# Sinkhorn attention with Fourier mixing on one core: an opening ranked by its longest path, and unread matmuls in TensorE's gaps

## Chip, cores and metric

The kernel runs on one core of a Trainium2 chip. The metric is the device time in microseconds (us) of one execution. Seven runs of the kernel before have a median of 299.0 us, from 294.36 to 301.5.

## What is computed

For 4 batches and 8 heads, a small 8x8 matrix per head is normalised five times by rows and columns (Sinkhorn). It mixes blocks of keys and values, attention runs within each block of 96 rows, and the result x (4 x 768 x 512) goes through a Fourier mixing and a two-layer MLP:

```python
for _ in range(5):
    P = exp(P - max(P)); P /= sum(P, axis=-1); P /= sum(P, axis=-2)
k_sorted = einsum('bhij,bhjcd->bhicd', P, k_b)
v_sorted = einsum('bhij,bhjcd->bhicd', P, v_b)
attn = softmax(scale * q_b @ k_sorted_b.T)       # within each block
x = attn @ v_sorted_b                            # heads side by side
u = x + real(fft(fft(x, axis=1), axis=2))
un = (u - mean(u)) / sqrt(var(u) + 1e-6)         # over the last axis
out = u + maximum(un @ w_ch1, 0) @ w_ch2
```

## The kernel before

The program is not written in the order in which it runs. Every step is recorded with `P.add` as an operation: the engines that may do it, a cost for each, what it reads and writes, a priority, and the buffers it opens. `Plan.schedule` (L201) then plays these costs forward, engine by engine: an engine takes the ready operation with the lowest priority number, and one that may run on ScalarE (ACT) or VectorE (DVE) goes to the engine that is free first. Loads over 32 KB are given a landing time from `HBM = 330.0` (KB per us) and `DLAT = 2.2`. The list of start times is sorted and the instructions are issued in that order. So the order on each engine is fixed when the kernel is built. On the chip each engine works through its list, and what stands first waits for its inputs while the rest of that list waits behind it.

The opening, for batch 0:

- Loads go out on GpSimd's queue (`load`, L395): k and q of the first four heads ("half 0"), v in two halves, k and q of half 1, then two constant tables; later the tables `cs` and `tab`, k and q of batch 1, the weights w1 and w2, v again for the second half of its rows, and k and q of batches 2 and 3. Small ones (`pack` with the identity, the Sinkhorn matrices) go out on SyncE's queue.
- Sinkhorn (L510 to L525) runs on DVE with five exponentials on ACT. Its result is spread to masks: `psk` (L542) and `bdk` (L547) for the keys, `bdv` (L656, L660) for the values.
- `v_path` (L586): 12 matmuls of 128x512 with the identity sum v over a block; L594 reduces that. `v_mix` (L635, L638): 16 groups of eight matmuls mix the values, and each is evicted to `vsf` (by the helper `copy`, L571) by ACT or DVE.
- `attn` for each pair of heads: `q_copy` and the transposes of q (L826, evicted at L571), `kqt` (L797, evicted to `ks`), `scores` (L851), exponential on ACT (L860), minus one (`em1`, L872 on DVE or L874 on ACT), `av` (L891, needs all 16 groups of `v_mix`), and normalisation on DVE (L902, L905) into `rt`.
- `a_path` (L675 to L747) makes correction rows, which three copies bring to `rb` (L760).
- `dft1` (L919 to L985): sums and differences on DVE (`pmt`, `eo`, `fo`), matmuls L952. `dft2` (L1005, L1012, six tiles of 128 rows, in two groups g of three): `u` (L1020), statistics (L1026, L1028), four small operations on GpSimd ("ln", L1033 to L1042), `un` (L1052, L1056), for batch 0 a transpose on TensorE (L1071) and an eviction into `ut`; for later batches a DMA transpose.
- `mlp(b, g)`: 16 groups of four matmuls 128x384 (L1091) with a ReLU eviction (L1100, L1103), then three tiles of 16 matmuls 128x512 (L1112), an addition into `u` (L1120) and a store of 256 KB on SyncE's queue. There are eight such tiles; this work has the lowest rank and fills TensorE (PE) wherever nothing else is ready.

Attention of batch 1 and `v_path(1)` have ranks between; they may be placed ahead of the first MLP tile too. [...] five in pool "pf", three in pool "pm". The MLP uses "pm".

```python
    at(-75.0, (v_path, (0,)))
    at(-60.0, (bdv_make, ()))
    at(-50.0, (v_mix, (0,)))
    at(-80.0, (attn, (0,)))
    at(-40.0, (a_path, (0,)), (a_rows, (0,)))
    at(-30.0, (dft1, (0,)), (dft2, (0, 0)), (dft2, (0, 1)))
    at(10.0, (make_bdk, (1,)), (attn, (1,)))
```

Of the kernel before, what the change touches and what calls it, by code (L numbers as in the profile page):

```python
# [10 lines left out]
F16 = mybir.dt.float16  # L11
# [10 lines left out]
DM = 512  # L22
# [3 lines left out]
RSC = 1.0 / XSC  # L26
YSC = 1.0 / 32.0
QB = (2, 3)
NK = 193
# [70 lines left out]
class Op:  # L100
    __slots__ = ("n", "costs", "fn", "preds", "succs", "left", "ready", "prio",
                 "vts", "fresh", "nbytes", "end", "start", "eng", "tag")

# [12 lines left out]
class Plan:  # L116
    HBM = 330.0
    DLAT = 2.2
# [12 lines left out]
    def add(self, costs, fn, r=(), w=(), prio=None, nbytes=0, tag="",  # L131
            after=()):
        o = Op()
        o.n = len(self.ops)
        o.costs, o.fn, o.nbytes, o.tag = costs, fn, nbytes, tag
        o.prio = self.prio if prio is None else prio
        o.preds, o.succs, o.vts, o.fresh = set(after), [], [], []
        for k in r:
            o.preds.update(self.wr.get(k, ()))
        for k in w:  # L140
            o.preds.update(self.wr.get(k, ()))
            o.preds.update(self.rd.get(k, ()))
        for k in r:
            self.rd.setdefault(k, []).append(o)
        for k in w:
            if self.rd.get(k):
                self.wr[k] = [o]
                self.rd[k] = []
            else:
                self.wr.setdefault(k, []).append(o)  # L150
        for k in list(r) + list(w):
            v = k if isinstance(k, Buf) else (
                k[0] if isinstance(k, tuple) and isinstance(k[0], Buf)
                else None)
            if v is None or v in o.vts:
                continue
            o.vts.append(v)
            v.users.append(o)
            if v.first is None:
                v.first = o  # L160
                o.fresh.append(v)
            elif v.first is not o:
                o.preds.add(v.first)
        o.preds.discard(o)
        self.ops.append(o)
        return o

    def schedule(self):
# [17 lines left out]
        def slot_time(o, held):  # L186
# [15 lines left out]
            return (None if short else t), short  # L202

        while todo:
            pick = None
            for e in free:
                t = free[e]
                cand = None
                soon = None
                held = set()  # L210
                for o in sorted(avail[e], key=lambda o: (o.prio, o.n)):
                    st = 0.0
                    if o.fresh:
                        st, short = slot_time(o, held)
                        if o.ready[e] <= t + 0.3:
                            held |= short
                        if st is None:
                            continue
                    s = max(o.ready[e], st)
                    if s <= t + 1e-9:  # L220
                        cand = o
                        break
                    elif soon is None or s < soon:
                        soon = s
# [69 lines left out]
def kernel(  # L294
# [97 lines left out]
    def load(dst, src, nbytes, w, prio, eng="POOL", r=(), after=()):  # L392
# [3 lines left out]
                     prio=prio, nbytes=nbytes, tag="load", after=after)  # L396


    slot = {}
    for b in range(B):  # L400
        for hf in range(2):
            base = (0, 4, 4, 0)[b]
            for n, nm in enumerate("kq"):
                slot[nm, b, hf] = base + 2 * hf + n

    def qk16(nm, b, hf):
        return kq[:, slot[nm, b, hf], :].rearrange(
            "p (h r d) -> p h r d", h=4, r=6)

    def load_qk(nm, b, hf, prio):  # L410
        src = {"k": k, "q": q}[nm]
        if nm == "q" and b in QB:
            for h in range(4):
# [3 lines left out]
                    src[b, 4 * hf + h].rearrange("(r p) d -> p r d", r=6),  # L417
                    196608, [("kq", slot[nm, b, hf])], prio + 0.01 * h)
            return
        load(kq[:, slot[nm, b, hf], :].rearrange("p (h x) -> p h x", h=4),  # L420
             src[b, 4 * hf:4 * hf + 4, :, :].rearrange(
                 "h (p r) d -> p h (r d)", r=6), 786432,
             [("kq", slot[nm, b, hf])], prio)

    def hk(g):
        return [("h", g, fc) for fc in range(16)]

    def load_v(t, hf, prio):
# [3 lines left out]
            [("nat", t, hf)] + (hk(0)[8 * hf:8 * hf + 8] if t == 0 else  # L432
                                [("kq", 2 * hf), ("kq", 2 * hf + 1)]), prio)

# [41 lines left out]
    for n, nm in enumerate(("pw", "pack", "vrow", "erow", "rrow")):  # L476
        load_c(nm, -500.0 + n, "SP")
    load_qk("k", 0, 0, -500.0)
    load_qk("q", 0, 0, -499.0)
    load_v(0, 0, -498.0)  # L480
    load_v(0, 1, -497.0)
    load_qk("k", 0, 1, -496.0)
    load_qk("q", 0, 1, -495.0)
    load_c("dtab", -494.0)
    load_c("lt", -493.0)
    load_c("cs", 19.0)
# [92 lines left out]
    def v_path(t):  # L579
        n3 = nat[t].rearrange("p (c d) -> p c d", d=D)  # L580
        psm = Buf("pm", "pf") if t else Buf("pm")
        stage = [("kq", n) for n in range(4)] if t else hk(0)
        for hf in range(2):
# [88 lines left out]
    def a_path(t):  # L672
        pa = Buf("pf")
        bd_, bp_ = Buf("qt"), Buf("qt")
        P.add(pe(0.4), lambda _: nc.tensor.matmul(  # L675
# [33 lines left out]
        px, pr = Buf("pf"), Buf("pf")  # L709
        hi, hi2 = Buf("qt"), Buf("qt")  # L710

# [7 lines left out]
        def f(_):  # L719
            for o in range(2):  # L720
                for par in range(2):
                    cc = slice(0, 129) if par == 0 else slice(129, 257)
                    for c in range(2):
# [7 lines left out]
              r=[pr], w=[hi], tag="rhi")  # L731
        P.add(evac(512), lambda e: copy(e, hi2.ap[0:64, 0:512],
                                        px.ap[0:64]),
              r=[px], w=[hi2], tag="rhi")
        for lo, hi_, o in ((0, 129, 0), (129, 257, 256)):
# [12 lines left out]
            rr[0:64, 1, :].rearrange("p (n m) -> p n m", n=2),  # L748
            hi2.ap[0:64, 0:512].rearrange("p (m n) -> p n m", n=2),
            nlo[0:64], px.ap[0:64].rearrange("p (m n) -> p n m", n=2),  # L750
# [3 lines left out]
    def a_rows(b):  # L754
        o = 32 * (b % 2)
        for dst, src in ((rb[0:32, :], rr[o:o + 32, 0, :]),
                         (rb[32:64, :], rr[64 + o:96 + o, 0, :]),
                         (rb[64:96, :], rr[o:o + 32, 1, :])):
            P.add({"SP": (0.1, 2.3)}, lambda _, dst=dst, src=src:
                  nc.sync.dma_start(dst, src),  # L760
                  r=[("rr", i) for i in (0, 1, 2, 3, 256)], w=["rb"],
                  tag="arow")
# [6 lines left out]
    def q_copy(b, hp):  # L769
# [9 lines left out]
        if not first:  # L779
            c["DVE"] = (0.28, 0.35)  # L780
        P.add(c, lambda e: copy(
            e, qr.ap.rearrange("p r (h d) -> p r h d", h=2), src),
            r=[("kq", slot["q", b, hf])], w=[qr], tag="qcp",
            after=[exps[-1]] if first else [])

    def kqt(b, hp):
# [4 lines left out]
        for half in range(2):  # L791
            ps = Buf("pf")

            def f(_, half=half, ps=ps):
                for r3 in range(3):
                    for h2 in range(2):
# [4 lines left out]
                            bdk[:, 2 * hp + h2].rearrange("p i c -> p (i c)"))  # L801
            P.add(pe(0.22), f, r=[("kq", slot["k", b, hf]),
                                  ("bdk", hp // 2)],
# [8 lines left out]
        if b in QB:  # L812
# [4 lines left out]
                kq[:, slot["q", b, hf], 768 * hl:768 * hl + 768]),  # L817
                r=[("kq", slot["q", b, hf])], w=[qt], tag="qX")
            return
# [60 lines left out]
    def av(b, h):  # L880
# [4 lines left out]
        def f(_):  # L885
            for T in range(6):
# [9 lines left out]
        P.add(pe(0.5), f, r=[(eb, 0), (eb, 1), "erow", "vrow", "vsz"]  # L896
              + [("vsb", n) for n in range(16)], w=[po], tag="av")
        rz = Buf("rz")
# [16 lines left out]
    def dft1(b):  # L915
        rt = rts[b]
        hs = [(rt, h) for h in range(H)]
        for n in range(2):
            P.add({"DVE": (0.86, 0.95)}, lambda _, n=n: V.tensor_tensor(  # L919
                pmt[:, 3 * n:3 * n + 3, 0:DM], rt.ap[:, 0:3, :],  # L920
                rt.ap[:, 3:6, :], op=ALU.add if n == 0 else ALU.subtract),
                r=hs, w=[("pm", n), ("fq", 0), ("fq", 1)],
                tag="pmt")
        P.add({"ACT": (0.17, 0.22)},
              lambda _: nc.scalar.copy(
                  pmt[:, :, DM:DM + 1], pmt[:, :, 0:1]),
              r=[("pm", 0), ("pm", 1)], w=["pm2"], tag="pmc")
        pms = [("pm", 0), ("pm", 1), "pm2"]
        P.add({"DVE": (0.88, 0.97)}, lambda _: V.tensor_tensor(
# [62 lines left out]
    def dft2(b, g):  # L992
# [4 lines left out]
        for tt in range(3):  # L997
# [11 lines left out]
            def f(_, one=one, ps=ps, T=T):  # L1009
                for c in range(4):  # L1010
# [5 lines left out]
                  r=[y4[c][g] for c in range(4)]  # L1016
                  + ["rb", "rrow", "lt", "lt96", "lt96a", "lt96b", "dtab"],
                  w=[ps, u], tag="dft2")
# [24 lines left out]
            nm.ap, nm.ap, -1.0, None, op0=ALU.mult), r=[nm], w=[(nm, 1)],  # L1043
            tag="ln")
        ut = Buf("ut")
        uts[b, g] = ut
        for tt in range(3):
# [20 lines left out]
            def f(_, un=un, pt=pt):  # L1068
                p16 = pt.ap.bitcast(F16)
                for c in range(4):  # L1070
# [9 lines left out]
                          "p (c s) -> p c s", c=4)),  # L1080
                  r=[pt], w=[(ut, tt, 1)], tag="utev")


# [43 lines left out]
    def attn(b):  # L1127
# [5 lines left out]
        for h in range(H):  # L1133
            av(b, h)

    def at(p, *fns):
        for fn, a in fns:
            P.prio = p
            fn(*a)
# [5 lines left out]
    at(-40.0, (a_path, (0,)), (a_rows, (0,)))  # L1145
    at(-30.0, (dft1, (0,)), (dft2, (0, 0)), (dft2, (0, 1)))
    at(10.0, (make_bdk, (1,)), (attn, (1,)))
# [18 lines left out]
    for b in range(B):  # L1166
        for g in range(2):
            mlp(b, g, 100.0 + 10 * (2 * b + g), -300.0)
    with tc.manual_schedule():
        for o in P.schedule():  # L1170
            o.fn(o.eng)
# [28 lines left out]
```

The softmax here doesn't subtract the row's maximum and nothing guards it: scores larger than these inputs give would overflow.

## Time and profile before

| | |
|---|---|
| median of seven runs | 299.0 us (294.36 to 301.5) |
| the profiled execution | 300.14 us, its span 298.4 us |
| PE busy | 269.8 us (90% of the span), 2332 matmuls |
| DVE busy | 177.8 us (60%); 56.70 us of the 65.40 from 10.00 to 75.40 |
| ACT busy | 153.5 us (51%) |
| mean granted TensorE clock | 0.971 |
| first MLP matmul (L1091) starts at | 75.39 us |
| PE busy from 133.80 to 294.50 | 160.55 us of 160.70 |

All times count from the first instruction of the span. "Busy" of PE counts pipelined matmuls that overlap. The granted clock (PEclk) is the share of TensorE's full clock in a stretch. A chain of waits is followed back from the last instruction to what released each step.

### The profile page before, as it was taken

Reading aid. Unit: us, or ns where it says so; the run is one execution under the profiler, and the core shown is the slowest. Engines: PE = TensorE matmul, PEld = TensorE weight load, DVE = VectorE, ACT = ScalarE, POOL = GpSimd, SP = SyncE. Lnnn points to the kernel's source line nnn. Section 1 sums busy time; section 2 is a strip of 40 time slices with the busy share of each in tenths; the row PEclk is TensorE's granted clock in tenths of the full one; section 3 lists DMA queues with packets and bytes.
Section 4 is the critical chain, followed back from the end, with each engine's and each line's share of the span. In section 5 each row is a group of like instructions: output and inputs, shape, how many; then the busy total and the mean of one; then the engine's idle time right before and its main releaser. Section 6 shows DMA issues by size and latency. Waiting matters only on the chain.

```text
span 298.4 us, 5829 instructions
## 1 busy us (share of the span) xinstructions
PE 269.8 (90%) x2332; PEld 165.0 (55%) x2332; DVE 177.8 (60%) x395; ACT 153.5 (51%) x307; POOL 54.7 (18%) x91
## 2 busy tenths in 40 slices
PE   0398978785999999889999999999999999999994
PEld 0264977664556565555556645545645645645641
DVE  5598589999699999776249954314605315312001
ACT  2476579863646897478237604513721631641710
POOL 8945312013800036030002000200200100010000
PEclk9999699996699999999999999999999999999999
DMA  7999999990910359625010210030021121121002
GB/s 115 218 283 218 216 206 213 204 118 13 71 12 2 72 98 165 134 13 108 35 71 15 55 70 35 20 107 36 15 53 70 37 53 70 37 54 70 37 0 105
DMA packets 43025, 26.32 MB, mean 88 GB/s; under 512 B 29834, under 2 KB 38552, under 8 KB 42996
## 3 DMA queue, kind: packets, MB, share of 16 engines
q0 software_dynamic: 22576, 15.16, 33.3%
q1 hardware_dynamic: 20422, 10.78, 12.4%
q8 instruction: 18, 0.29, 0.4%
q14 instruction: 9, 0.07, 0.1%
HBM read 28.95 MB, written 6.29 MB: 118 GB/s over the span
## 4 chain that ended last, share of the span: by engine, by line
PE 73%; DVE 15%; DMA 6%; POOL 2%; ACT 2%; issue 2%; DVEq 0%; ACTq 0%; POOLq 0%
PE bank L1112 28%; PE bank L1091 25%; DMA hr<-in_v_dram 4%; PE bank L635 3%; DVE rt L905 2%; PE bank L1005 2%; PE bank L952 2%; PE bank L851 2%; DMA out_dram<-u 2%; PE bank L891 2%; PE bank L586 2%; DVE pmt L919 2%; PE bank L638 2%; PE bank L797 1%; DVE u L1020 1%
## 5 line engine op out<-in xcount | busy, mean ns | idle before, releaser
L1103 ACT ACTIVATE hr<-bank 128x384 f16<-128x384 f32 x111 | 54.2, 490 | 80.1 <-PE bank L1091 79.8
L1091 PE MATMUL bank<-ut,w1sb 128*128 128x384 f16 x512 | 93.4, 331 | 0.8 <-DVE hr L1100 0.8
L1112 PE MATMUL bank<-w2sb,hr 128*128 128x512 f16 x384 | 88.9, 379 | 0.0
L1091 PEld LDWEIGHTS <-w1sb 128*128 128x128 f16 x512 | 49.5, 99 | 36.0 <-issue 3.0
L1112 PEld LDWEIGHTS <-hr 128*128 128x128 f16 x384 | 36.5, 98 | 40.5
L1120 DVE TENSOR_TENSOR u<-bank,u 128x512 f32<-128x512 f32 x24 | 16.6, 691 | 51.7 <-PE bank L1112 51.3
L1020 DVE SCALAR_TENSOR_TENSOR u<-rt,bank 128x512 f32<-128x512 f16 x24 | 16.1, 678 | 35.4 <-PE bank L1012 29.7
L860 ACT ACTIVATE ex<-bank 96x384 f32<-96x384 f32 x64 | 27.9, 485 | 7.3 <-PE bank L851 5.5
L1033 POOL TENSOR_SCALAR mv<-mv 128x3 f32<-128x3 f32 x8 | 2.6, 320 | 142.2 <-DVE mv L1028 140.0
L1052 ACT ACTIVATE un<-u,nm,ny 128x512 f16<-128x512 f32 x14 | 11.4, 811 | 14.2 <-POOL nm L1042 8.5
L395 POOL DMA_DIRECT2D kq<-in_q_dram x20 | 17.5, 892 | 5.3 <-ACT vsf L571 1.9
L891 PE MATMUL bank<-vsf,eb 97*128 97x65 f16 x384 | 15.8, 195 | 2.7 <-DVE u L1020 1.3
L874 ACT ACTIVATE eb<-ex,negone 96x384 f16<-96x384 f32 x29 | 17.5, 614 | 0.2
L905 DVE TENSOR_TENSOR rt<-bank,rz 128x384 f16<-128x384 f32 x32 | 17.3, 549 | 0.4
L891 PEld LDWEIGHTS <-eb 97*128 97x128 f16 x384 | 14.3, 98 | 4.8 <-issue 2.9
L826 PE MATMUL bank<-pack,qr 128*128 128x128 f16 x48 | 4.9, 252 | 12.6 <-ACT qr L571 11.8
L1026 DVE BATCH_NORM_STATS2 st<-u 128x6 f32<-128x512 f32 x24 | 15.9, 682 | 0.2
L571 ACT CAST vsf<-bank 96x512 f16<-96x512 f32 x19 | 13.9, 786 | 4.1 <-PE bank L638 3.2
L395 POOL DMA_DIRECT2D kq<-in_k_dram x8 | 6.5, 810 | 48.4 <-issue 27.7
L635 PE MATMUL bank<-bdv,vcx 128*128 128x128 f16 (+1 forms) x128 | 14.0, 236 | 1.1 <-ACT bdv L571 1.1
L872 DVE TENSOR_SCALAR eb<-ex 96x384 f16<-96x384 f32 x35 | 13.1, 376 | 1.2 <-ACT ex L860 0.9
L1100 DVE TENSOR_SCALAR hr<-bank 128x384 f16<-128x384 f32 x17 | 9.4, 551 | 5.6 <-PE bank L1091 5.6
(114 smaller groups left out, 336.7 us busy)
## 6 DMA issues: line engine op xcount, KB each, us to landing
out_dram<-u SPq DMA_DIRECT2D x24, 256.0 KB, 2.0
kq<-in_k_dram POOLq DMA_DIRECT2D x8, 384.0 KB, 9.3
w1sb<-in_moe_w_ch_dram POOLq DMA_DIRECT2D x4, 512.0 KB, 15.2
w2sb<-in_moe_w_ch_dram POOLq DMA_DIRECT2D x4, 512.0 KB, 18.8
kq<-in_q_dram POOLq DMA_DIRECT2D x4, 384.0 KB, 11.2
hr<-in_v_dram POOLq DMA_DIRECT2D x2, 768.0 KB, 12.5
kq<-in_v_dram POOLq DMA_DIRECT2D x2, 768.0 KB, 21.3
kq<-in_q_dram POOLq DMA_DIRECT2D x16, 96.0 KB, 6.0
```

Of the source, the lines that this page charges most:

```text
L395: return P.add({eng: c}, lambda _: e.dma_start(dst, src), r=r, w=w, prio=prio, nbytes=nbytes, tag="load", after=after)
L635: nc.tensor.matmul(o, vcx[:, 96 * d:96 * d + m], bd, start=True, stop=(t == 1))
L860: nc.scalar.activation(ex.ap, pss[h2].ap[0:96, 0:384], AF.Exp, scale=SCALE),
L874: nc.scalar.activation(ed, src, AF.Identity, bias=negone[0:96])
L891: nc.tensor.matmul(po.ap[:, 65 * T:65 * T + 65], eb.ap[:, e0:e0 + 128], vsf[:, vi:vi + 65], start=(n == 0), stop=(n == 1), skip_group_chec ...
L905: P.add({"DVE": (0.45, 0.56)}, lambda _: V.tensor_tensor(rt.ap[:, :, D * h:D * h + D], po3()[:, :, 0:D], rz.ap[:, :, None].broadcast_to([1 ...
L1020: V.scalar_tensor_tensor(u.ap.rearrange("p (m n) -> p m n", n=2), rt.ap[:, T, :].rearrange("p (m n) -> p m n", n=2), RSC, ps.ap.rearrange( ...
L1026: P.add({"DVE": (0.6, 0.69)}, lambda _, u=u, st=st: V.bn_stats(st.ap, u.ap), r=[u], w=[st], tag="bn")
L1091: nc.tensor.matmul(ps.ap[:, 0:GT], w1sb[:, c, 128 * fc:128 * fc + 128], ut.ap[:, c, :], start=(c == 0), stop=(c == 3))
L1103: nc.scalar.activation(hr[g][:, fc, :], ps.ap[:, 0:GT], AF.Relu)
L1112: nc.tensor.matmul(ps.ap, hr[g][:, fc, 128 * tt:128 * tt + 128], w2sb[:, fc, :], start=(fc == 0), stop=(fc == 15))
L1120: V.tensor_tensor(u.ap, ps.ap, u.ap, op=ALU.add),
```

## The change

1. Ranking. `aim(goal)` walks back from `goal`, the last operation that `dft2(0, 0)` returns (the eviction of its third tile into `ut`). Every operation on which it depends gets the priority -1000 minus the length of the longest path from it to the goal; loads keep theirs. The first loads get numbers near -5000 so that they stay first. `dft2(0, 1)` follows at -29.
2. Planner. `HBM` goes from 330 to 400. Which buffers are held back for a waiting operation of better rank is decided over all engines and not for each. `LOOK` is empty, so the branch that it guards is never entered.
3. Filling. An empty operation opens a "pm" bank (`spin`) at the start, and another closes it after the goal. When the instructions are issued, the gaps that the plan has on PE ahead of the goal are filled with matmuls of 128x480 (identity times the bits of `pack`) into that bank, one for each 0.22 us of a gap. Nothing reads the bank.
4. Finer dependencies: q and k by head (`kqk`), the three rows of `rb` each by itself, `pmt` in halves of 256 columns (four DVE operations for two).
5. Buffers of `a_path` move from the pool `qt` to `un`, `yr` and `ex`.
6. Loads of q and k for batches 2 and 3 wait for the second "ln" (that of `dft2(0, 1)`).

```diff
+SPIN = 0.22
+LOOK = {}
...
-    HBM = 330.0
+    HBM = 400.0
...
+    def aim(self, goal):
+        def best(o):
+            return min(c[1] for c in o.costs.values()) + self.XL
+        tail = {goal: 0.0}
+        for o in reversed(self.ops):
+            if o in tail:
+                for p in o.preds:
+                    tail[p] = max(tail.get(p, 0.0), tail[o] + best(o))
+        for o, t in tail.items():
+            o.crit = True
+            if o.nbytes == 0:
+                o.prio = -1000.0 - t
...
+            want = {}
+            for e in free:
+                for o in avail[e]:
+                    if o.fresh and o.ready[e] <= free[e] + 0.3:
+                        for p in slot_time(o, ())[1]:
+                            want[p] = min(want.get(p, o.prio), o.prio)
...
-                        st, short = slot_time(o, held)
-                        if o.ready[e] <= t + 0.3:
-                            held |= short
+                        st, short = slot_time(
+                            o, [p for p in want if want[p] < o.prio])
...
+    spin = Buf("pm")
+    P.add({"PE": (0.001, 0.001)}, lambda _: None, w=[spin], prio=-9000.0,
+          tag="spin")
...
     def load_qk(nm, b, hf, prio):
+        after = lns[1:2] if b > 1 else ()
...
-        bd_, bp_ = Buf("qt"), Buf("qt")
+        bd_, bp_ = Buf("un"), Buf("un")
...
-        hi, hi2 = Buf("qt"), Buf("qt")
+        hi, hi2 = Buf("yr"), Buf("ex")
...
-    at(-30.0, (dft1, (0,)), (dft2, (0, 0)), (dft2, (0, 1)))
+    at(-30.0, (dft1, (0,)))
+    goal.append(dft2(0, 0))
+    at(-29.0, (dft2, (0, 1)))
...
     with tc.manual_schedule():
+        P.aim(goal[0])
+        P.add({"PE": (0.001, 0.001)}, lambda _: None, r=[spin],
+              after=[goal[0]], prio=-2000.0, tag="spun")
+        t = 3.5
         for o in P.schedule():
+            if o.eng == "PE":
+                if o.start < goal[0].end:
+                    for _ in range(int((o.start - t - 0.05) / SPIN)):
+                        nc.tensor.matmul(
+                            spin.ap[:, 0:480], idh,
+                            pack.bitcast(F16))
+                t = max(t, o.start + o.costs["PE"][0])
             o.fn(o.eng)
```

What this makes of the lists: 56 such matmuls stand on PE, 23 ahead of everything, 10 between the first two groups of q transposes, 9 between the two halves of `v_path(0)`, and 14 singly or up to three at a time from the end of `v_mix(0)` to the last transposes ahead of the first MLP tile. The order of nearly every operation ahead of that tile changes on PE, ACT and DVE.

## Prediction

> **What bounds the kernel now.** I read the page's slices first, then busy time in stretches of 2.5 us, then the chain of waits in order of time, then single lines.
>
> ```profile
> PE   0398978785999999889999999999999999999994
> DVE  5598589999699999776249954314605315312001
> PEclk9999699996699999999999999999999999999999
> ```
>
> A slice is 7.46 us. From slice 18 on (134 us) PE is full, 160.55 of 160.70 us, at full clock: only less work could shorten that, and the change removes none. What can change lies ahead. Near 30 to 37 us and 67 to 82 us the granted clock falls below 0.9. From about 42 to 75 us DVE is full.
>
> ```profile
> 67.50:70.00 2.50, 1.19 (x19) 0.91 (x19) 2.50 (x7) 0.00 (x0) 0.51 (x2) 0.87 0.05 13
> 70.00:72.50 2.50, 1.12 (x16) 0.96 (x16) 2.38 (x6) 0.81 (x1) 1.07 (x3) 0.50 0.10 26
> 75.00:77.50 2.50, 2.50 (x14) 1.29 (x14) 1.56 (x4) 2.50 (x6) 2.50 (x4) 0.50 0.09 8
> 77.50:80.00 2.50, 2.50 (x13) 1.43 (x12) 1.11 (x3) 0.34 (x2) 2.50 (x4) 0.58 1.66 111
> 122.50:125.00 2.50, 1.41 (x13) 0.87 (x13) 2.22 (x8) 0.81 (x2) 0.00 (x0) 1.00 0.78 156
> 132.50:135.00 2.50, 1.75 (x12) 0.88 (x10) 1.01 (x2) 1.91 (x4) 0.21 (x1) 1.00 0.12 22
> ```
>
> The columns are stretch, length, busy us (instructions) of PE, PE's weight loads, DVE, ACT and GpSimd, clock, DMA share, GB/s. PE waits for the first MLP tile from 65 us on and loses half its clock; the tile then starts cold, and DVE waits for it (1.56 and 1.11 of 2.50). Later PE is short of work twice.
>
> ```profile
> 75.46 3.95 PE bank L1091 x12
> 117.16 5.51 DMA out_dram<-u
> 122.78 0.69 DVE u L1020
> 129.96 0.88 POOL kq L395
> 130.86 1.25 POOL ny L1036
> 284.00 10.37 PE bank L1112 x48
> ```
>
> In the chain, twelve L1091 take 3.95 us (329 ns each) in the cold; a later run of 28 takes 4.55 us (162.5 ns). The two shortages have names: a store that takes 5.51 us holds the buffer of `u`, and a q load (0.88 us) stands between two "ln" operations on GpSimd.
>
> ```profile
> L586 PE MATMUL bank<-hr,pack x12: 584/631/634, 13.9 to 23.5; 128*128 128x512 f16 x12
> L586 PE MATMUL bank<-kq,pack x12: 377/379/389, 82.1 to 86.0; 128*128 128x512 f16 x12
> ```
>
> The same matmul takes 631 ns up to 24 us and 379 ns later: PE is cold from its first instruction until then too, though the page's clock says 1.00 there (I take it that no event was recorded yet).
>
> [...] from the 0.87 and 0.58 above, the cold stretch runs from 69.35 to 79.6 us[...], and L1091 doubles. [...] the fifth Sinkhorn exponential, behind a q copy on ACT that waits 1.99 us for its load, starts at 11.03 us.
>
> **The change, part by part.**
>
> *Filling.* 56 matmuls of 480 columns. Their price is not in the trace: between L1091 (384 columns, 162.5 ns) and L1112 (512 columns, 10.37/48 = 216 ns) I estimate 203 ns warm, and double, 0.41 us, cold. `pack` lands near 3.3 us (issue 1.18 plus 2.1). The 23 first ones then take 4.7 us (all warm) to 9.4 us (all cold); [...] The first q transposes cannot start before 11.1 us (load 10.29, copy 0.83). Cost 0 to 0.3 us; I take 0, covered by the q load. The next 10 and 9 (3.9 us warm) fall between 11.6 us and v's second half, which lands by 17.85 us (a GpSimd issue is released by it there). The first half costs 6 x 0.216 = 1.3 us warm. Cost 0; if PE were cold, 3.9 us more, on the path. The 14 later ones (2.8 us) lie where PE is idle 0.3 us or more in each 2.5 us: 0, or up to 1.0 us if they stand ahead of something ready.
>
> *Order of the opening.* In the new list all `kqt` stands behind q transposes of half 1, and on DVE `bdk` behind a q copy of half 1. That half lands at 21.75 us (the GpSimd issue there waits for it). Copy 0.82, transposes 0.5: `kqt` starts near 23.1 us, where it started at 18.2. In return `psk`, `bdv` and the sum of v are not held behind cold L586 (2.72 us each half), and `v_mix` follows the first scores, near 25.4 us, where it was 30.17. Ahead of it PE has little to do from 19 to 25 us, so it falls cold again: I take 5 us cold, as before (30.2 to 35.2). A group is eight matmuls of 107 ns cold, 55 warm: 5.8 groups in 5 us, 10.2 groups by 0.44 = 4.5 us, and 1.6 us for scores, `kqt` and transposes between. End near 36.5 us; before, DVE goes on at 41.37.
>
> From there to the last DVE eviction of `ut`, before, DVE is full for 31.9 us (41.37 to 73.27). The new list has more in it: 4 `ks` (0.47), 1 q eviction (0.87), 1 `bdk` (1.1), 2 L905 (0.47), 3 L902 (0.11), 1 `un` (0.46), 1 aggregate (0.09), `pmt` in halves about equal; less: 2 `em1` (0.27), 4 and 2 steps of `a_path` (0.17, 0.18). Durations are distances between starts where DVE is full. Sum 1.88+0.87+1.1+0.94+0.33+0.46+0.09-0.54-1.04 = +4.1, so 36.0 us. 36.5+36.0+2.1 (from that eviction to L1091, as before) = 74.6 against 75.4: **-0.8 us**. Bounds: -3 (PE warm in `v_mix` saves 2.5 there), +4 (`v_mix` ends as late as before).
>
> *Clock at the first MLP tile.* Twelve matmuls of `v_path(1)` (2.6 us) come ahead of the tile, right behind `dft2`, with five fillers (1.0 us). PE is then dense until about 3 us before the tile[...]. I take it warm: 3.95/2 = **-2.05 us**; bounds 0 and -2.5.
>
> *Later.* With the tile warm and `v_path(1)` done, its store comes earlier against the loads of batch 3, with which it collides: at most the 5.51 less a usual 2.0; I take what PE is idle there (1.09 and 0.11): **-1.2**, bounds -3.5 and +2. In the new list all twenty loads of batches 2 and 3 stand ahead of the "ln" of `dft2(1, 0)`, so no load parts it: 0.88 at most, I take **-0.6** of PE's 0.75 idle. These loads start at 76 us, not 48; attention of batch 2 transposes q from 97.6 us on: 0. SyncE's list is the same in kind and order. Finer dependencies and other buffers: 0, seen only in the order.
>
> Sum -0.8-2.05-1.2-0.6 = -4.65: span 298.4 to 293.75, its execution 300.14 to 295.5. The median of the runs is 1.1 lower than that execution, so I forecast 299.0-4.65 = **294.4 us**.
>
> **Rivals.**
>
> *The clock falls all the same.* [...] Then -0.8-1.2-0.6: 296.4. [...] Against: the 3.6 us of dense matmuls.
>
> *Given back.* Batch 1's chain is DVE's (busy 9.79 of 10 us from 80 to 90), not PE's. A sooner, warmer tile only drains the stock of MLP work, and PE idles longer at 120 to 134 us. Only the -0.8 stays: 298.2. Against: from 91 to 117 us the chain is PE's.
>
> *Slower: the opening stands behind the late half.* `kqt`, `bdk` and the `ks` evictions wait for q's second half, 4.9 us later than before; only four exponentials, not eight, are done ahead of `v_mix`, and DVE's tail is 4.1 us longer. It decides when the last `vsf` eviction comes after 37.3 us (41.4-4.1). If it comes at 41 again, the tile starts near 79, with PE idle and cold ahead of it: +3.5, 302.5. For it: the +4.1 is counted from the list. Against: `v_mix` starts 4.8 us earlier.
>
> **Chances.** Likeliest case 0.46 (its own range 290 to 297), clock falls 0.17, given back 0.20, late half 0.17. The range, 290 to 301, leaves out two in ten, mostly of the last case and of a warm `v_mix`. A measurement here can tell about 1%: faster is below 296.0, slower above 302.0. Faster 0.41+0.08+0.06 = 0.55; slower 0.15; within 0.30.
>
> **What would show it.** Right: L586 at first near 380 ns; a first L635 near 25 us; L1091 starting at 73 to 76 us with 162 ns between matmuls; DVE full again at 75 to 80; no q load ahead of L1036's counterpart at 125 to 132. Wrong: kqt far past 23 us, the last `vsf` eviction after 40, clock 0.5 at the tile, or PE idle over 3 us between 115 and 135.

## The result, and the profile after

The changed kernel takes 299.0 us (median of 23 runs, 296.25 to 300.6), the kernel before 298.2 us (median of 60 runs, 294.01 to 302.22). The comparison gives a ratio of 1.0096, 95% interval 1.0071 to 1.0121: slower by about 1%, where 294.4 was forecast. The ratio leaves out the runs of the kernel before that lie more than 1.5% above its fastest, 27 of 60, and none of the changed kernel's, which is why it is larger than the ratio of the two medians, 1.003. By either number the gain that was forecast is not there. The profiled execution took 298.69 us, its span is 296.8 us, its mean granted clock 0.982.

The page's slices of the kernel after:

```profile
PE   5979988998959998799999999999999999999994
DVE  4678999999947997795249866214705215312001
PEclk9997999999978999999999999999999999999999
```

A slice is now 7.42 us. PE works from the start (the filler matmuls). The slow clock that was at 67 to 82 us is gone from there; the 7 in slice 11 and the 8 in slice 12 (counted from 0) lie at 82 to 96 us, and PE's slice 11 is a 5. Again in stretches of 2.5 us (columns as in the prediction):

```profile
67.50:70.00 2.50, 2.11 (x32) 1.43 (x31) 2.50 (x9) 2.47 (x6) 1.11 (x2) 1.00 0.00 0
70.00:72.50 2.50, 2.40 (x18) 1.40 (x17) 2.50 (x6) 2.25 (x5) 2.28 (x4) 1.00 0.03 3
75.00:77.50 2.50, 2.50 (x37) 1.61 (x33) 2.50 (x8) 1.94 (x6) 2.50 (x4) 1.00 2.26 160
77.50:80.00 2.50, 2.50 (x28) 1.99 (x24) 2.46 (x8) 1.85 (x5) 1.52 (x2) 1.00 1.55 191
82.50:85.00 2.50, 0.00 (x0) 0.00 (x0) 1.03 (x3) 0.37 (x1) 0.00 (x0) 0.93 1.41 129
85.00:87.50 2.50, 2.02 (x14) 1.02 (x15) 0.09 (x1) 0.86 (x2) 0.00 (x0) 0.50 0.46 102
122.50:125.00 2.50, 0.98 (x10) 0.52 (x10) 1.72 (x6) 1.00 (x3) 0.00 (x0) 1.00 1.49 114
132.50:135.00 2.50, 2.50 (x26) 1.27 (x25) 2.50 (x6) 2.36 (x7) 0.00 (x0) 1.00 0.94 81
```

From 67.5 to 80 us the aim is met: the clock is 1.00 and DVE, which had waited at 75 to 80 us (1.56 and 1.11 busy), is full. The first MLP matmul (L1158, before L1091) starts at 69.75 us against 75.39. Then PE does nothing at all from 82.5 to 85 us and goes on at half its clock. The chain of waits has the reason:

```profile
78.16 7.28 DMA qt<-kq
85.48 0.50 PE bank L911 x8
85.98 2.67 PE bank L1158 x8
...
125.46 1.63 POOL ny L1101
```

PE's timeline names what it stood at, and GpSimd's when the loads behind it were issued (the last bracket is idle time and who ended it):

```profile
85.48 0.50 PE L911 MATMUL bank<-qt,ks 64*128 64x96 f16 x8 [3.61 <-DMA qt<-kq]
```

```profile
70.83 0.86 POOL L442 DMA_DIRECT2D kq<-in_k_dram  x1
71.70 3.30 POOL L442 DMA_DIRECT2D kq<-in_q_dram  x4
74.95 0.80 POOL L442 DMA_DIRECT2D kq<-in_k_dram  x1
75.69 3.33 POOL L442 DMA_DIRECT2D kq<-in_q_dram  x4
```

These ten are the loads of k and q for batch 2, which the change makes wait for the second "ln". The kernel before issued two of k and two of q between 40.87 and 61.94 us, but the other six of q from 75.21 us on, the last of them later than the last here. What moved is their reader, the DMA transposes of this q on SyncE's queue. Before:

```profile
75.21 5.66 POOL L395 DMA_DIRECT2D kq<-in_q_dram  x6
97.62 7.50 SPq L815 DMA_TRANSPOSE qt<-kq  x4
```

After:

```profile
78.16 13.26 SPq L874 DMA_TRANSPOSE qt<-kq  x4
```

The new list has attention of batch 2 some 19 us earlier, so that the first transpose runs while q's second half is still being loaded. It lands 7.28 us after its issue (the chain's line above), where the transposes of q in the kernel before take 2.7 us (median). With 2.7 us it would have landed near 80.9 us, ahead of 81.87 us, when PE came to the scores; that is an estimate from these figures. The scores L911 stand first on PE, and eight MLP matmuls (L1158, next in the chain) stand behind them: none of the eight started in the 3.61 us that PE stood idle. Within this gap the clock is halved, from 84.66 us to 91.48 us (0.93 in the mean from 82.5 to 85 us, 0.50 from 85 to 90, 0.70 from 90 to 92.5).

### The profile page after: what moved, and what is told of

It reads as the page before. It is cut to its first block, busy times and chain, and to the rows that moved or that the text cites. A ratio compares the mean times of both kernels' runs of the same rounds, so it can differ in the third digit from the quotient of the medians.

```text
span 296.8 us, 5946 instructions
## 1 busy us (share of the span) xinstructions
PE 277.0 (93%) x2388; PEld 165.8 (56%) x2388; DVE 176.2 (59%) x400; ACT 155.1 (52%) x310; POOL 54.5 (18%) x91
## 4 chain that ended last, share of the span: by engine, by line
PE 68%; DVE 12%; DMA 8%; issue 5%; POOL 4%; ACT 3%; DVEq 0%; POOLq 0%; ACTq 0%
PE bank L1179 27%; PE bank L1158 26%; DMA kq<-in_q_dram 5%; PE bank L1017 3%; POOL kq L442 2%; DMA qt<-kq 2%; PE bank L1070 2%; PE bank L692 2%; DVE rt L966 2%; PE bank L911 2%; ACT ex L920 1%; PE bank L695 1%; PE bank L856 1%; PE bank L1077 1%; PE bank L951 1%
## 5 line engine op out<-in xcount | busy, mean ns | idle before, releaser
L1170 ACT ACTIVATE hr<-bank 128x384 f16<-128x384 f32 x106 | 52.0, 491 | 87.0 <-PE bank L1158 86.1
L1158 PE MATMUL bank<-ut,w1sb 128*128 128x384 f16 x512 | 95.3, 331 | 0.1
L1158 PEld LDWEIGHTS <-w1sb 128*128 128x128 f16 x512 | 48.3, 99 | 34.5 <-issue 1.7
L934 ACT ACTIVATE eb<-ex,negone 96x384 f16<-96x384 f32 x38 | 22.6, 610 | 0.1
L1249 PE MATMUL bank<-pack 128*128 128x480 f16 x56 | 14.9, 397 | 3.3 <-DMA pack<-k_pack 3.3
L911 PE MATMUL bank<-qt,ks 64*128 64x96 f16 x256 | 12.4, 215 | 4.6 <-DMA qt<-kq 3.6
L442 POOL DMA_DIRECT2D kq<-in_q_dram x20 | 16.4, 849 | 1.7 <-DMA kq<-in_q_dram 1.2
L1167 DVE TENSOR_SCALAR hr<-bank 128x384 f16<-128x384 f32 x22 | 12.0, 549 | 7.6 <-PE bank L1158 7.4
L1091 DVE BATCH_NORM_STATS2 st<-u 128x6 f32<-128x512 f32 x24 | 15.9, 682 | 0.2
L911 PEld LDWEIGHTS <-ks 64*128 64x128 f16 x256 | 7.5, 98 | 11.1 <-issue 6.0
L856 PE MATMUL bank<-bdk,kq 128*64 128x128 f16 x192 | 10.9, 226 | 2.5 <-DVE u L1085 1.5
```

Of the source, the lines that this page charges most:

```text
L442: return P.add({eng: c}, lambda _: e.dma_start(dst, src), r=r, w=w, prio=prio, nbytes=nbytes, tag="load", after=after)
L911: nc.tensor.matmul(pss[h2].ap[:, BLK * j:BLK * j + BLK], ks.ap[rows, 4 * g + j, :], qt.ap[rows, c0:c0 + BLK])
L934: nc.scalar.activation(ed, src, AF.Identity, bias=negone[0:96])
L1091: P.add({"DVE": (0.6, 0.69)}, lambda _, u=u, st=st: V.bn_stats(st.ap, u.ap), r=[u], w=[st], tag="bn")
L1158: nc.tensor.matmul(ps.ap[:, 0:GT], w1sb[:, c, 128 * fc:128 * fc + 128], ut.ap[:, c, :], start=(c == 0), stop=(c == 3))
L1170: nc.scalar.activation(hr[g][:, fc, :], ps.ap[:, 0:GT], AF.Relu)
```

## Experiments

My theory after this reading: the held loads (part 6 of the change), met by an order that needs them early, take back what the opening wins. The rivals: the new opening wins less than it seems and the ranking costs it later on; or the fillers, and the bank that they take, cost more than the clock that they keep. All kernels compute the whole of the reference. Ratios are to the kernel before on the same chip, with 95% intervals.

**Held loads, alone.** All lists are those of the changed kernel, but on GpSimd the ten loads of batch 2 are issued early.

```diff
-        for o in P.schedule():
+        todo = P.schedule()
+        for o in [o for o in todo if o.tag == "ld2"]:
+            todo.remove(o)
+            last = max(todo.index(p) for p in vls + list(o.preds)
+                       if p is not lns[1])
+            todo.insert(last + 1, o)
+        for o in todo:
```

> The changed kernel with the same lists on TensorE, ACT, DVE and SyncE; on GpSimd's queue alone the ten loads of k and q of batch 2 stand right behind the two v loads, as soon as their slots are free, ahead of the ln operations. Theory (held loads): the stall of 3.6 us at 81.9 to 85.5 and the cold 6.8 us behind it go, 3.6 + 3.4 = about 7 us: span near 290 to 291, ratio to before about 0.98. Rival (batch 1's chain on DVE bounds 75 to 130 us anyway): the time comes back as idle TensorE at 115 to 130 us, and the span stays within 2 us of 296.8. Second rival (the DMA transposes are slow by themselves): the stall stays at 85 us.

Measured: 294.5 us, ratio 0.9927 (0.9896 to 0.9957), span 291.1 us. The loads are now issued between 40.37 and 63.4 us, the last of them the second one of k, and L915 (the same scores) finds its operands:

```profile
62.65 0.77 POOL L442 DMA_DIRECT2D kq<-in_k_dram  x1
```

```profile
82.34 0.34 PE L915 MATMUL bank<-qt,ks 64*128 64x96 f16 x8
```

There is no bracket: PE did not wait. It starts 3.14 us earlier, the cold stretch at 85 us is gone (one of 3.4 us comes at 111.8 us), and the second MLP tile starts at 106.3 us instead of 111.8. The span is 5.7 us shorter although the first MLP tile starts 0.6 us later (70.35). Nothing else differs between the two kernels, so the place of these loads costs the changed kernel about 1.7% (1.0096 against 0.9927). The span came out as expected; the ratio did not fall to 0.98.

**The hold left out**, and everything planned anew.

```diff
-        after = lns[1:2] if b > 1 else ()
+        after = ()
```

> The changed kernel without the hold on the loads of batches 2 and 3, planned anew. Held-loads theory: no wait for a q transpose, 290 to 293. Rival (order of the plan, not the hold): another order is planned, and it ends within 2 us of 296.8.

Measured: 294.7 us, ratio 0.9943 (0.9909 to 0.9976), span 290.9 us; first MLP matmul at 72.83 us, PE idle 2.3 us in all after it (6.5 in the changed kernel, gaps above 0.3 us). This agrees. The first tile starts 3.1 us later than in the changed kernel, but that is not simply the price of loading early: with the same lists, early loads cost 0.6 us there (the experiment above), and the order planned anew puts 36 more matmuls ahead of the tile.

**The fillers left out**, lists the same.

```diff
-                    for _ in range(int((o.start - t - 0.05) / SPIN)):
+                    for _ in range(0):
```

> The changed kernel with all 56 unread matmuls left out; the lists are otherwise the same, and the bank stays held. If the fillers keep the clock up: the early v_path matmuls go back from about 380 to 630 ns, the first MLP matmuls start cold in most executions, and the span is 1 to 3 us longer. If they cost more than they give: 0 to 1 us shorter. The stall at 82 us stays in both.

Measured: 300.0 us, ratio 1.0138 (1.008 to 1.0197), span 298.9 us. The first MLP matmul starts at 71.38 us, and the tile is warm without fillers too (clock 1.00 from 70 to 72.5 us): the cold stretches are 21.1 to 28.0, 86.0 to 92.8 and 126.9 to 130.4 us. The wait at L911 stays (3.3 us). With the wait for the loads gone as well:

> The changed kernel with the ten loads of q and k of batch 2 issued early on GpSimd, as in early_q (ratio 0.9927), and without the 56 filler matmuls. All lists otherwise the same. Theory fillers are worth what no_fill showed (about 2 us): ratio 0.998 to 1.002, first MLP matmul 71.4. Rival, the fillers' worth in no_fill came from the cold stretch at 127 us behind the stall and not from the opening: with the stall gone their worth falls below 1 us, ratio 0.992 to 0.996.

Measured: 293.9 us, ratio 0.9936 (0.9907 to 0.9966), first MLP matmul at 71.58 us. Against 0.9927 with fillers that is no difference. In the new order the fillers bring the tile forward by 1.2 to 1.6 us, and what is left of that at the end is too little to be told apart.

**The ranking left out**, planned anew; by the same rule for the gaps, 69 fillers now stand on PE and not 56.

```diff
-        P.aim(goal[0])
```

> The changed kernel without the ranking by longest path (the walk back from the goal is left out), planned anew with everything else. If the ranking makes the first MLP tile early: it starts near 74 us again, not 69.75. The end depends on whether the q transposes of batch 2 are waited for: if yes 299 to 302, if they come later in the list 294 to 296.

Measured: 293.5 us, ratio 0.9902 (0.9871 to 0.9932), span 290.1 us. The tile was expected near where it was before; it starts at 69.89 us, within 0.14 us of the changed kernel's. So with the rest of the change in place the ranking is not what brings it forward. (The finer dependencies, the moved buffers and the new choice of which buffers are held were not left out singly.) Ranking starts `v_mix` 3.7 us earlier (24.1 against 27.8), but of that 2.1 us are left at the last eviction to `vsf` (34.40 against 36.48) and 0.14 at the MLP. The loads of batch 2 are issued at the same times here (from 70.62 us), yet PE waits less:

```profile
85.03 0.34 PE L911 MATMUL bank<-qt,ks 64*128 64x96 f16 x8 [0.80 <-DMA qt<-kq]
```

In this order other work of batch 1 stands ahead of the scores. The stall needs both, the late loads and an order that reaches them with nothing left in front. Two more kernels leave out the ranking and also the hold (`after = ()`), or the ranking with the ten loads issued early, as in the first experiment:

> The changed kernel without the ranking and without the hold on the loads of batches 2 and 3, replanned; fillers, the rate of 400, finer buffers and smaller dependencies are kept. Theory: each of the two parts alone gave back time when it was left out (ratios 0.9902 and 0.9943), but without the ranking the transposes of q of batch 2 were hardly waited for any more (0.8 us), so leaving out the hold as well adds little: ratio 0.986 to 0.991. Rival, they add up (the hold costs 5 us in any order): ratio 0.975 to 0.983. Rival, early loads compete with the opening again: ratio over 0.995, first MLP matmul after 72.

> The changed kernel without the ranking (ratio 0.9902), and with the ten loads of q and k of batch 2 issued right behind the second half of v(1) on GpSimd. Lists otherwise identical to no_rank. Theory: no_rank waits for them only 0.8 us, so the ratio stays at 0.987 to 0.991. Rival, the loads still delay what follows without a wait that shows: ratio below 0.986. Rival, no better than 0.992, since early loads compete with the opening.

Measured: 293.4 us, ratio 0.9901 (0.9867 to 0.9935), and 293.5 us, ratio 0.9865 (0.9803 to 0.9927). The parts do not add up; with 0.8 us of waiting there is little left to win, and the two can't be told from 0.9902.

**Fillers on the kernel before**: 82 of them, one "pm" bank set aside, nothing else of the change. Beside it the same lists and bank without the 82 matmuls.

```diff
+    spin = Buf("pm")
...
+            if o.eng == "PE":
+                if o.start < goal[0].end:
+                    for _ in range(int((o.start - t - 0.05) / SPIN)):
+                        nc.tensor.matmul(
+                            spin.ap[:, 0:480], idh,
+                            pack.bitcast(F16))
```

> The kernel before with the filler matmuls alone: one bank of PSUM set aside for them, the lists replanned with a bank less, 82 fillers where the planner sees PE idle ahead of the first second-step DFT matmul; nothing else of the change. Theory clock (the cold 6.8 to 10.2 us around the first MLP tile are worth some 2 us): the tile is warm, its first matmul stays within 1 us of 75.4, ratio 0.992 to 0.996. Theory fillers are worth nothing here (the tile becomes warm by the denser order, not by fillers): ratio 0.998 to 1.002. Rival, the bank that is lost costs more than the clock gives: ratio over 1.002. If the fillers were also what brings the first MLP tile forward by 5.6 us, its first matmul would lie near 70.

> The kernel fill_before (ratio 0.9936, first MLP matmul 71.3) with the same lists and its bank set aside, but without the 82 filler matmuls. Theory fillers: without them the time is that of the kernel before, ratio 0.998 to 1.004, a cold stretch of 6.8 us or more around the first MLP tile, its first matmul near 75. Rival, the lists planned with a bank less are what is better: ratio 0.992 to 0.996 again, first MLP matmul near 71 to 72.

Measured: with fillers 293.9 us (292.65 to 295.36), ratio 0.9936 (0.9914 to 0.9958), first MLP matmul at 71.3 us; without them 299.1 us, ratio 1.0073 (1.004 to 1.0106), first MLP matmul at 76.39 us. The lists are the same, so in the order of before the fillers are worth 1.4%, about 4 us. They bring the tile forward by 5.1 us, where the theory had it within 1 us of 75.4, and nearly to where the whole change has it. (The two profiles are of runs of 292.69 and 301.74 us, so part of the 5.1 us may be the spread of the runs.) In twelve of the fourteen profiles of this study the tile starts 33.4 to 35.7 us after the last eviction to `vsf`; what differs is when that eviction ends, from 34.40 to 41.64 us. The stretch with the first MLP matmuls, without fillers and with them:

```profile
75.00:77.50 2.50, 2.34 (x23) 1.29 (x22) 1.96 (x6) 2.35 (x6) 2.33 (x4) 0.50 0.00 0
```

```profile
72.50:75.00 2.50, 2.50 (x22) 1.67 (x21) 2.41 (x6) 2.50 (x7) 2.50 (x4) 1.00 0.91 61
```

The clock is 0.50 in the one and 1.00 in the other. The lists planned with a bank less cost 0.7% by themselves, more than was expected.

**The planner's rate on the kernel before**, alone and with the fillers.

```diff
-    HBM = 330.0
+    HBM = 400.0
```

> The kernel before with one number changed: the planner's HBM rate is 400 instead of 330, lists replanned. Since the changed kernel without its ranking still starts the first MLP tile at 69.9 us, something else brings it forward. Theory rate (loads counted as landing sooner move transposes and QK up in the lists): first MLP matmul near 70 to 72, ratio about 0.985 to 0.995. Rival (the finer buffers, smaller dependencies and the new choice of who holds a buffer do it): first MLP matmul within 1.5 us of 75.4, ratio 0.995 to 1.005.

> The kernel before with the fillers and the planner's rate of 400, nothing else of the change, replanned. Alone, fillers gave 0.9936 and the rate 0.9899 with a wide interval. Theory, they act in different places (the clock of the opening; the order after the first MLP tile): ratio 0.980 to 0.988. Rival, both recover the same few us: ratio 0.988 to 0.993. If it is below 0.988 it is the fastest kernel of this study.

Measured: alone 292.5 us (6 runs), ratio 0.9899 (0.9843 to 0.9954); with fillers 293.5 us, ratio 0.987 (0.9809 to 0.993). The rate was expected to bring the first tile forward, and it does not: the tile starts at 75.15 us in the profile of the first and at 73.43 us in that of the second, 71.3 us with fillers and the old rate. What the rate does is to bring attention of batch 2 forward: the first DMA transpose of its q starts at 69.91 us, and at 69.04 us with the fillers, where fillers and the old rate have 91.50 us. So the rate alone, in the order of before, is enough for the early demand that the changed kernel's hold then meets; what the buffers moved out of the pool `qt` add to it was not tried. Nothing holds the loads here, and PE does not wait for these transposes. The first profile is of its slowest run, 296.62 us, so where the median's gain lies stays open, and so does whether the two add up.

**The kernel before, profiled again.**

> The kernel before, unchanged, profiled once more, since its runs spread from 294 to 302 us and the profile used so far lies at the upper end (span 298.4). Theory clock: a profile with a shorter span has its first MLP tile partly or wholly warm, so the difference sits between 69 and 80 us (up to 5 us) and its first MLP matmul stays near 75. Rival, another wait sets the spread: the first MLP matmul itself lies 2 us or more earlier or later, or the gaps of PE after 100 us differ.

Measured: 296.25 us, span 294.5 us. The first MLP matmul starts at 72.65 us, 2.74 us earlier than in the profile that the forecast was made from. From about 30 us on the two differ; first this profile, then the earlier one:

```profile
30.00:32.50 2.50, 2.50 (x49) 2.50 (x47) 2.28 (x4) 2.18 (x3) 0.85 (x2) 1.00 1.20 222
...
70.00:72.50 2.50, 1.97 (x25) 1.33 (x23) 2.42 (x9) 2.26 (x5) 1.54 (x5) 0.50 0.00 0
```

```profile
30.00:32.50 2.50, 2.33 (x23) 2.33 (x23) 1.51 (x2) 1.10 (x3) 0.82 (x2) 0.50 1.21 221
```

`v_mix` ran warm here (49 matmuls in a stretch against 23), so the rival of this expectation holds for the place, and the clock is the likely cause all the same: `v_mix` starts 0.7 us earlier here, and its last eviction ends 3.1 us earlier. The first MLP tile is cold in both.

## Why the prediction was wrong

The opening was forecast too cautiously, and the step of "Later" on the held loads, taken as 0, cost more than the forecast gain. The steps in their order:

- *Filling, cost 0*: right. The 23 first fillers take 6.21 us, from 3.31 us on (forecast: 4.7 to 9.4 us, from near 3.3), and the first q transposes follow at 9.62 us; the 11.1 us given as the earliest for them was wrong, without harm. Nine fillers take 1.99 us with the 0.366 us of the last one, so their starts lie 203 ns apart, as estimated. The first half of `v_path` is warm:

```profile
L643 PE MATMUL bank<-hr,pack x12: 376/378/379, 12.7 to 17.5; 128*128 128x512 f16 x12
L643 PE MATMUL bank<-kq,pack x12: 378/379/389, 62.4 to 65.2; 128*128 128x512 f16 x12
```

In the kernel before the medians of these two rows were 631 and 379 ns.

- *Order of the opening, -0.8*: right in kind, wrong in size; the tile starts 5.64 us earlier, outside the bound of -3. `kqt` starts at 21.41 us (forecast 23.1), `v_mix` at 24.08 (25.4), the cold stretch is 3.4 us (5), the last `vsf` eviction ends at 34.40 us (36.5). From there to the MLP it takes 35.35 us against 34.7 before; the +4.1 that I counted from the list of DVE turned out as +0.65. So the tile starts 4.85 us sooner than forecast, 2.1 by the end of `v_mix` and 2.75 by the tail. That it takes the ranking is refuted: without it the tile starts at 69.89.
- *Clock at the first MLP tile, -2.05*: right, though that PE would stay warm was only an estimate. Twelve L1158 take 2.37 us of PE, 4.02 before, so -1.65. But not by fillers alone: without them it is warm too (1.00 from 70 to 72.5 us).
- *Store against the loads of batch 3, -1.2*: wrong. Those loads are issued from 107.86 us on, beside the stores again; PE's gaps after 115 us are 0.86, 1.54 and 0.54 us, 2.94 in all, where they were 1.88.
- *No q load parts "ln", -0.6*: the mechanism is right (the four operations run from 125.15 to 127.69 us with nothing between), the gain is not there, because "u" ahead of them is late: PE's 1.54 us end with it.
- *"These loads start at 76 us, not 48; attention of batch 2 transposes q from 97.6 us on: 0"*: this is the step that failed. The loads did start late, at 70.83 us, but "not 48" reads the old trace by its first load of k alone: six of the eight q loads started from 75.21 us on there. The 97.6 us were read from the old trace too, though the lists had changed; in the new one the transposes begin at 78.16 us, into the loads, and the first takes 7.28 us. It cost the wait of 3.61 us and up to 3.0 us of half clock while PE ran behind it (85.48 to 91.48), two thirds of the 9.9 us that the opening had won (the first three terms below). Moving these loads alone gives a span 5.7 us shorter.

The balance of the two profiled spans: first tile -5.64, its clock -1.65, twelve matmuls of `v_path(1)` done ahead of it (0.216 us each) -2.6, the wait +3.6, the clock behind it at most +3.0, later gaps +1.1: -2.2 us against -1.6 measured; the 0.6 us between them are not accounted for. That the runs nevertheless come out slower has a second cause: the profile that I started from was a long one. Half of the gain at the first tile, 2.74 of 5.64 us, the kernel before has by itself in a run of 296.25 us whose `v_mix` is warm. The distance to the median (1.1 us) that the forecast took off did not cover this. So the held loads are not the whole miss: with them early the ratio is 0.9927, where the forecast of 294.4 for 299.0 means 0.985.

The rivals: *Given back* named 298.2 us, the nearest number, but by another mechanism (PE short of work at 120 to 134 us); the loss is at 82 to 91 us. *The clock falls* did happen, not at the first tile but in the wait. *The opening stands behind the late half* did not: the last `vsf` eviction ended well before the 37.3 us from which it decides. No rival had the held loads. What I named as proof of error, over 3 us idle between 115 and 135, nearly came (2.94); the gap that mattered was in none of my stretches.

## What to carry to other kernels

When a scheduler re-orders a kernel, a time from the old trace for when some operand is needed is void: for every load that a change holds back, find its first reader in the new list of each engine, and what work of that engine stands in front of it. The wait at the head of TensorE's list cost its length here and a slow clock behind it (3.61 us and up to 3.0 us). Change one thing at a time: here the unread matmuls alone gave 0.6% and the change without its ranking 1%, and all parts together lost them.

## What the runs showed that was not expected

The kernel before spreads over 8 us (294.01 to 302.22) with one and the same program. Two profiles of it differ in whether `v_mix` ran warm. With the fillers 21 runs lie within 2.7 us.

The clock in a profile can say 1.00 where PE is cold. In the kernel before with a bank less:

```profile
32.50:35.00 2.50, 2.50 (x27) 2.50 (x25) 1.42 (x2) 0.99 (x2) 0.74 (x1) 1.00 1.05 211
35.00:37.50 2.50, 2.50 (x46) 2.50 (x45) 1.73 (x3) 2.02 (x3) 0.54 (x1) 1.00 1.06 213
```

Both stretches show 1.00, but with PE full it does 27 matmuls in the first and 46 in the second; the starts of the 128-column matmuls are 107 ns apart up to 35.2 us, then 56. By that pace PE was cold up to there, and so a mean clock of 0.985 goes with a span of 300.0 us.

The clock also fell without a long gap. With the ten loads early it falls at 111.79 us (0.7 in the page's slice from 109.2 to 116.4 us), where the longest gap of PE shortly before was 0.86 us, against 3.61 us in the changed kernel. So the length of a single gap does not tell here when the clock falls; what does was not shown.

The loads of q moved little while the DMA engines were full. From 75 to 77.5 us of the changed kernel the DMA share is 2.26 at 160 GB/s (the times of packets that overlap add up, so it can exceed 1); from 17.5 to 20 us it is 1.26 at 270 GB/s. In the first of these stretches 2651 of 2720 packets are under 512 B, in the second 30 of 582; from 68 to 88 us, those of the transposes included, it is 8704 of 9731. The first three transposes of q run beside these loads: the first lands after 7.28 us, the third after 3.8 us. Whether the small packets are the cause, and whether larger ones would help, was not tried.
